# Batch 2's second projection with the weights held still and its result turned by DMA, in a kernel whose whole order is one table, laid anew

## The chip, the cores and the metric

The kernel runs on one core of a Trainium2 chip. The metric is device time in microseconds (us) of one execution. Before the change it is 368.34 us, the median of three runs (368.06 to 368.48).

## What is computed

Attention over 8 batches, 12 heads, 448 positions and 64 values a head, with a denominator that has one extra term; then a gated long convolution over the 448 positions, and a last projection:

```python
scores = q @ k^T / 8
e = exp(scores - max)
attn = e / (sum(e) + exp(-max) + 1e-9)
x = heads side by side of (attn @ v)              # (8, 448, 768)

proj = x @ w_proj                                 # (8, 448, 2304)
x1, x2, x3 = three parts of 768 columns
x2_conv = irfft(rfft(x2) * rfft(filter_fft))      # over the 448 positions
out = (x1 * x2_conv * x3) @ w_out                 # (8, 448, 768)
```

Inputs and output are float32; the kernel computes in bf16 with float32 sums.

## The kernel before

**Attention.** The work runs over 48 head pairs, i = 0 to 47, six for each batch. For a pair, K and Q must stand transposed (tiles kT and qT). In batches 0 and 1 ("staged") this goes: a load of each of k, q and v on SP's queue (L492, L497), casts to bf16 on GpSimd (L519 for k, L525 for q, L532 for v), seven transposes on TensorE (L558 for the shared remainder of K, L560 for k, L567 for q; one group "T" a pair), and copies out of PSUM on VectorE (L577, L588). From batch 2 on ("loaded") the casts go into the tile nat, and DMA transposes on SP's queue (L628, L635) fill qT and kT. The scores come from L867 (two heads side by side on 64 rows each) and L869 (the remainder), the exponentials from ScalarE (L880 and L886), and the sums over v from L898 (remainder) and L906. VectorE divides (L919 to L921) into the tile xb. The tile wout_bf serves as room for the exponentials of pairs 2 and 5 before w_out is loaded into it; so "wout_bf" in an instruction of the first 30 us means pair 2 or 5.

**Dense work of a batch.** xb is transposed into xT (L973 by DMA, L982 on TensorE in batch 0). The gates x1 and x3 are 72 matmuls of 448 columns (L1197). For x2, VectorE folds xT into sums and differences (tile xf, L1046 and L1051), since the transform is done as real matrices on folded halves. Then the second projection has two forms:

- `proj2` (L1074): the folded data is the stationary operand, the weights move: 8 groups (4 parts of the spectrum, 2 halves of the columns) of 6 matmuls with 384 columns. Positions lie on the partitions, as the transform that follows needs them. Each group is copied out of PSUM, on ScalarE (L1088) or VectorE (L1086).
- `still2` (L1096): the weights are the stationary operand and all four parts of the folded data move past them at once: 6 groups of 6 matmuls with 456 columns. The result has channels on the partitions. It is copied out (L1109 on ScalarE, L1107 on VectorE) and turned by two DMA transposes on SP's queue (`turn2`, L1113), of three groups each.

The tuple TURNED (L334) names the batches that use the second form: 3 to 7. The room that the copies write is the batch's own xb for the batches that are not in WHOLE, which are those before 5. After it come the transform (L1149 for the first form, L1145 for the second), the product with the filter's spectrum, the inverse (L1244), the gating, and the last projection (L1010), whose results ScalarE copies out (L1319) and SP stores (L1326, L1329).

**What sets the order.** Every step is a task, added with `plan.add`: engine, estimated cost, what it needs and makes. `Plan.run` plays the tasks through with these estimates. ORDER, a table with one number for each task, in the sequence in which the tasks are added, sorts each engine's tasks; each engine executes its own in that order, and waits where an input is missing. The constants at the head of Plan (L52 to L72: LANDING, DELAY, EARLY, TURN_ROOM and others) are its estimates of transfers. With ORDER given, what is played through decides two things: which of the eight PSUM banks a task gets, and where "fillers" stand: runs of small matmuls on zeros (L1483, method `fillers`) that the plan puts into gaps of TensorE which it expects in the first 44 us:

```python
count = int(self.FILL[2] * (at - end) / 0.056) if end >= self.COLD[0] else -int((end - at) // self.COLD[1])
```

GpSimd also issues the loads of weights: the filter (L761 to L765), w_proj in parts (L845) and w_out (L850).

Of the kernel before, what the change touches and what calls it, by code (L numbers as in the profile page):

```python
# [41 lines left out]
class Plan:  # L42
# [11 lines left out]
    LANDING = 1.89  # L54
    DELAY = (0.87, 3.1)
    EARLY = ((3.0, -0.56), (13.0, 0.95))
    TURN_ROOM = 0.55
# [3 lines left out]
    ORDER = ()  # L61
    OPEN = 8
# [19 lines left out]
    def add(self, eng, cost, want, emit, need=(), make=(), take=(), give=(), dma=0.0, run=256, n=1, after=0.0, begun=(), late=0.0, turn=False, part=None, keep=False, port=False, rows=128):  # L82
        want = self.ORDER[len(self.tasks)] if self.ORDER else want + self.SHIFT.get(part, 0.0)
        if eng == "SP":
            dma *= self.STRETCH
        if eng == "DVE" and port:
            cost += self.SHARED
        self.tasks.append((want, len(self.tasks), eng, cost, emit, need, make, take, give, dma, after, run, n, begun, late, turn, keep, port or eng == "POOL" and not dma, rows))

    def run(self):  # L90
# [37 lines left out]
        def over():  # L128
            return sum(h[1] for h in queues["SP"] if h[2][15]) - self.TURN_ROOM if begin else 0.0

# [7 lines left out]
        def transfers(to):  # L138
            nonlocal clock
            while clock < to:  # L140
# [11 lines left out]
                for e, h in heads.items():  # L152
                    h[1] -= step * h[2][11] / total
                    if h[1] <= 1e-9:
                        queues[e].pop(0)
                        landed[e].extend([clock + self.LANDING + h[2][14]] * h[2][12])
                        done(h[2], clock + self.LANDING + h[2][14], "SP")
            release()
# [60 lines left out]
        while any(queue.values()):  # L219
            moved = False  # L220
            for e in queue:
# [33 lines left out]
                if t[9]:  # L255
                    q = queues["POOL" if e == "POOL" else "SP"]
                    if t[15]:

                        begin[t[1]], free[e] = end, 1e9
                    early, more = self.EARLY[e == "POOL"]  # L260
                    q.append([now + self.DELAY[e == "POOL"] + (more if now < early else 0.0), t[9], t])
                    q.sort(key=lambda h: h[0])
# [53 lines left out]
def kernel(  # L316
# [17 lines left out]
    TURNED = (3, 4, 5, 6, 7)  # L334
# [86 lines left out]
    def stage(g, at, n):  # L421
# [4 lines left out]
    plan = Plan(  # L426
        {
            "e": 6, "er": 2, "e3": 3, "er3": 1, "k0": 2, "q0": 2, "u": 1, "w": 1, "xf": 1,
            "x2": 1, "x2s": 1, "x2b": 2, "xs": 2, "t0": 2, "t1": 2, "yh": 1, "g": 1, "x1": 2, "cr": 2, "cw": 1, "cv": 2, "yT": 1, "yR": 1,
            "os": 3,  # L430
        }
    )
# [1031 lines left out]
    with (  # L1464
# [56 lines left out]
        for (part, ch), at in zip(LOADS, LOAD):  # L1521
# [4 lines left out]
            elif ch is None:  # L1526
                add("POOL", 0.82, at, lambda part=part: wproj_load(part, None), make=[("w", part, 0), ("w", part, 1)], dma=4.9,
                    run=115, late=-0.34, after=at)
# [13 lines left out]
    with (  # L1542
# [6 lines left out]
        for b in range(n_batches):  # L1549
            W["yT", b], W["yR", b // 2] = y, yr  # L1550
            stable(b)
            plan = Plan(plan.size)
# [9 lines left out]
    with tc.manual_schedule(engines={E.PE, E.Pool, E.DVE, E.Activation, E.SP}):  # L1562
        plan = main
# [31 lines left out]
```

## Time and profile before

| | |
|---|---|
| time, median of 3 runs | 368.34 us |
| lowest and highest | 368.06, 368.48 us |
| the profiled execution's own time | 371.93 us |
| its span | 370.1 us |
| TensorE busy | 359.4 us (97%) |
| ScalarE, VectorE, GpSimd busy | 262.3, 259.7, 112.0 us |
| granted clock of TensorE, mean | 0.995 |

The span runs from the first to the last instruction; 1.8 us of the execution's own time lie outside it. That execution took 3.6 us more than the median of the others, so durations read from it are those of a slightly slower run. Names stand as written tile, arrow, read tiles; PE is TensorE, PEld its weight loads, ACT ScalarE, DVE VectorE, POOL GpSimd, SP the engine that issues most transfers; a "q" behind the name marks the engine's instruction sequencer.

### The profile page before, as it was taken

Reading aid. Unit: us, or ns where it says so; the run is one execution under the profiler, and the core shown is the slowest. Engines: PE = TensorE matmul, PEld = TensorE weight load, DVE = VectorE, ACT = ScalarE, POOL = GpSimd, SP = SyncE. Lnnn points to the kernel's source line nnn. Section 1 sums busy time; section 2 is a strip of 40 time slices with the busy share of each in tenths; the row PEclk is TensorE's granted clock in tenths of the full one; section 3 lists DMA queues with packets and bytes.
Section 4 is the critical chain, followed back from the end, with each engine's and each line's share of the span. In section 5 each row is a group of like instructions: output and inputs, shape, how many; then the busy total and the mean of one; then the engine's idle time right before and its main releaser. Section 6 shows DMA issues by size and latency. Waiting matters only on the chain. (4 is left out here: it accounts for less than half of the span.)

```text
span 370.1 us, 9355 instructions
## 1 busy us (share of the span) xinstructions
PE 359.4 (97%) x3612; PEld 215.7 (58%) x3612; DVE 259.7 (70%) x671; ACT 262.3 (71%) x453; POOL 112.0 (30%) x247
## 2 busy tenths in 40 slices
PE   8879999999999999999999999999999999999995
PEld 6557666556755675655565555655555556565653
DVE  7547589894798578793586768784478858767570
ACT  6958777776887768877687766888588784465523
POOL 7582453224560354435217144410120000000000
PEclk9989999999999999999999999999999999999999
DMA  8999999987997999899999999879952055135125
GB/s 195 263 240 218 218 201 221 206 189 181 227 223 204 247 319 200 204 200 235 228 209 256 255 229 240 220 173 234 220 111 44 2 87 105 67 95 120 43 91 173
DMA packets 132163, 68.41 MB, mean 185 GB/s; under 512 B 88781, under 2 KB 128656, under 8 KB 132112
## 3 DMA queue, kind: packets, MB, share of 16 engines
q1 hardware_dynamic: 127392, 62.11, 73.9%
q0 software_dynamic: 4480, 5.41, 8.6%
q8 instruction: 29, 0.48, 0.5%
q10 hardware_dynamic: 240, 0.23, 0.3%
q14 instruction: 22, 0.18, 0.2%
HBM read 43.86 MB, written 11.01 MB: 148 GB/s over the span
## 5 line engine op out<-in xcount | busy, mean ns | idle before, releaser
L880 ACT ACTIVATE e<-psum 128x896 bf16<-128x896 f32 x138 | 122.2, 922 | 30.2 <-PE psum L867 29.5
L1197 PE MATMUL psum<-xT,wproj_bf 128*128 128x448 bf16 x576 | 121.5, 352 | 0.0
L1197 PEld LDWEIGHTS <-wproj_bf 128*128 128x128 bf16 x576 | 53.9, 98 | 47.7 <-issue 4.2
L1010 PE MATMUL psum<-wout_bf,yT 128*128 128x384 bf16 x288 | 54.0, 326 | 0.1
L906 PE MATMUL psum<-vn,e 128*128 128x65 bf16 x1104 | 44.3, 194 | 0.0
L906 PEld LDWEIGHTS <-e 128*128 128x128 bf16 x1104 | 39.4, 98 | 6.7 <-issue 3.0
L867 PE MATMUL psum<-qT,kT 64*128 64x448 bf16 x288 | 42.6, 357 | 0.1
L664 POOL CAST nat<-nat 112x512 bf16<-112x512 f32 x36 | 23.2, 651 | 62.8 <-DMA nat<-in_q_dram 62.5
L1157 ACT CAST xs<-psum 113x384 bf16<-113x384 f32 (+1 forms) x64 | 29.2, 486 | 17.5 <-PE psum L1145 10.8
L1319 ACT COPY osb<-psum 128x384 f32<-128x384 f32 x56 | 25.7, 489 | 18.8 <-PE psum L1010 11.1
L1163 DVE TENSOR_TENSOR t<-xs,hrs 113x768 bf16<-113x768 bf16 (+1 forms) x64 | 37.7, 612 | 1.7 <-ACT xs L1157 1.6
L1010 PEld LDWEIGHTS <-yT 128*128 128x128 bf16 x288 | 27.3, 98 | 18.4 <-issue 1.1
L1096 PE MATMUL psum<-xf,wproj_bf 128*128 128x456 bf16 x180 | 37.5, 356 | 0.0
L921 DVE TENSOR_TENSOR xb<-psum,den 128x512 bf16<-128x512 f32 x48 | 33.2, 691 | 1.7
L1213 DVE TENSOR_TENSOR g<-x,psum 128x448 bf16<-128x448 bf16 x42 | 25.8, 616 | 10.3 <-PE psum L1197 7.7
L1211 ACT CAST x<-psum 128x448 bf16<-128x448 f32 x42 | 22.3, 541 | 10.9 <-PE psum L1197 9.9
L1253 ACT CAST cr<-psum 128x452 bf16<-128x452 f32 x48 | 24.7, 549 | 7.5 <-PE psum L1244 7.0
L886 ACT ACTIVATE er<-psum 128x448 bf16<-128x448 f32 x46 | 25.3, 556 | 4.1 <-PE psum L869 4.0
L684 POOL CAST nat<-nat 128x384 bf16<-128x384 f32 x29 | 16.0, 558 | 39.2 <-DMA nat<-in_k_dram 33.5
L1074 PE MATMUL psum<-wproj_bf,xf 128*113 128x384 bf16 x144 | 27.1, 328 | 0.0
L1096 PEld LDWEIGHTS <-wproj_bf 128*128 128x128 bf16 x180 | 17.0, 98 | 16.3 <-issue 1.5
L919 DVE TENSOR_SCALAR den<-psum 128x8 f32<-128x8 f32 x48 | 7.9, 164 | 25.0 <-PE psum L906 23.6
(136 smaller groups left out, 491.8 us busy)
## 6 DMA issues: line engine op xcount, KB each, us to landing
nat<-in_q_dram SPq DMA_DIRECT2D x47, 224.0 KB, 4.5
out_dram<-osb SPq DMA_DIRECT2D x23, 384.0 KB, 3.6
nat<-in_k_dram SPq DMA_DIRECT2D x41, 192.0 KB, 4.5
nat<-in_v_dram SPq DMA_DIRECT2D x41, 192.0 KB, 4.5
wproj_bf<-in_moe_w_proj_dram POOLq DMA_DIRECT2D x2, 1152.0 KB, 12.2
out_dram<-osb SPq DMA_DIRECT2D x10, 192.0 KB, 3.2
rests<-in_k_dram SPq DMA_DIRECT2D x8, 192.0 KB, 4.2
rests<-in_v_dram SPq DMA_DIRECT2D x8, 192.0 KB, 4.8
```

The source lines that it names most:

```text
L867: nc.tensor.matmul(sc[:, u, 0:S], kT[b % 2][c, hp, t, :], qT[b % 2][c, hp, :])
L880: nc.scalar.activation(to, of, AF.Exp, scale=SCALE)
L906: nc.tensor.matmul(out_bank(u)[:, n, :], P["e"][1 + t][:, u * S + n * 128 : u * S + n * 128 + 128], vn[b % 2][:, hp, 4 * u + t, :], start= ...
L921: nc.vector.tensor_tensor(W["xb", b][:, hp].rearrange("p n (u d) -> p u n d", u=2), op[:, :, :, 0:DH], rec[:].unsqueeze(3).to_broadcast([1 ...
L1010: nc.tensor.matmul(ops[:n, :DCH], y[:, dt, 0:n], wout_bf[:, dt, ch * DCH : (ch + 1) * DCH], start=(dt == 0), stop=(dt == NDT - 1),)
L1074: nc.tensor.matmul(pps[:FQ, :DCH], W["xf", b][:, kt, pg, 0:FQ], wproj_bf[:, kt, D + ch * DCH : D + (ch + 1) * DCH], start=(kt == 0), stop= ...
L1096: nc.tensor.matmul(pps, wproj_bf[:, kt, D + dt * 128 : D + (dt + 1) * 128], W["xf", b][:, kt], start=(kt == 0), stop=(kt == NDT - 1),)
L1157: nc.scalar.copy(L["xs", par, ch][:K, pg % 2, :], L["Z", pg, ch][:K, :DCH])
L1163: nc.vector.tensor_tensor(t[:K], L["xs", par, ch][:K], h, op=ALU.mult)
L1197: nc.tensor.matmul(p[:, :S], wproj_bf[:, kt, 2 * part * D + dt * 128 : 2 * part * D + (dt + 1) * 128], xT()[:, kt, 0:S], start=(kt == 0), ...
L1213: nc.vector.tensor_tensor(g[:, dt, :], L["x1", dt], p[:, :S], op=ALU.mult)
L1319: nc.scalar.copy(L["os", st][:n, ch * DCH : (ch + 1) * DCH], L["O", st, ch][:n, :DCH])
```

## The change

Three things are changed. Batch 2 joins TURNED, so its second projection is of the second form: `still2` and two DMA transposes for `proj2`. The estimates of transfers are renewed: four constants, and a table TIMES that gives 254 tasks, those that start transfers, a cost, transfer time, weight and lateness of their own. And ORDER has new numbers throughout (2,134 for 2,136, since batch 2 has other tasks).

```diff
-    LANDING = 1.89
-    DELAY = (0.87, 3.1)
-    EARLY = ((3.0, -0.56), (13.0, 0.95))
-    TURN_ROOM = 0.55
+    LANDING = 1.738
+    DELAY = (0.917, 3.66)
+    EARLY = ((3.0, -0.67), (13.0, 0.95))
+    TURN_ROOM = 1.05
...
+    TIMES = {}
...
+        cost, dma, run, late = self.TIMES.get(len(self.tasks), (cost, dma, run, late))
         self.tasks.append((want, len(self.tasks), eng, cost, emit, need, make, take, give, dma, after, run, n, begun, late, turn, keep, port or eng == "POOL" and not dma, rows))
...
-    TURNED = (3, 4, 5, 6, 7)
+    TURNED = (2, 3, 4, 5, 6, 7)
...
-    plan.ORDER = (2, 0, 1, 152, 3, 4, 0, 0, 2, 1, 3, 4, 2, 9, 32,
...
+    plan.ORDER = (2, 0, 2, 167, 3, 4, 0, 0, 2, 1, 3, 4, 3, 1, 30,
...
+    plan.TIMES = {3: (0.64, 0.05, 256.0, 0.0), 15: (0.58, 0.735, 50.0, 0.1807), 16: (0.58, 1.17, 50.0, -0.1523),
...
```

Lines behind L437 move down by 4: L845 becomes L849. In the main part TensorE has 48 matmuls of L1074 less and 36 of L1096 more, and 78 fillers where there were 72. VectorE loses four copies of L1086 and gets three of L1107, ScalarE loses four of L1088 and gets three of L1109, and SP gets two DMA transposes of L1113 more.

**GpSimd, from the cast of k for pair 3 on.** L519 is a cast of k, L525 one of q, each for the next pair in turn; L532 is one of v. Before:

```order
L519 CAST ldm<-nat 128x2x3x64
L525 CAST ldm<-nat 112x2x4x64
L761 DMA filt<-in_moe_filter_fft_dram 112x4x768
L762 DMA filt<-in_moe_filter_fft_dram 1x3x768
L765 DMA filt<-in_moe_filter_fft_dram 1x16x48
L525 CAST ldm<-nat 112x2x4x64
L532 CAST vn_93<-nat 128x3x64 x2
L519 CAST ldm<-nat 128x2x3x64 x2
L525 CAST ldm<-nat 112x2x4x64
L845 DMA wproj_bf<-in_moe_w_proj_dram 128x6x768
```

The cast of q right behind the filter's loads is pair 4's, and the two casts of k further on (x2) are those of pairs 4 and 5. After:

```order
L529 CAST ldm<-nat 112x2x4x64 x2
L536 CAST vn_93<-nat 128x3x64 x4
L556 CAST vn_93<-rests 128x6x64
L765 DMA filt<-in_moe_filter_fft_dram 112x4x768
L766 DMA filt<-in_moe_filter_fft_dram 1x3x768
L769 DMA filt<-in_moe_filter_fft_dram 1x16x48
L523 CAST ldm<-nat 128x2x3x64
L536 CAST vn_93<-nat 128x3x64 x2
L849 DMA wproj_bf<-in_moe_w_proj_dram 128x6x768
L536 CAST vn_93<-nat 128x3x64 x2
L523 CAST ldm<-nat 128x2x3x64
L529 CAST ldm<-nat 112x2x4x64 x2
```

The cast of k for pair 3 (the first L523 here) now stands behind the filter's loads, that of pair 4 (the second) ahead of its q, and the first load of w_proj ahead of pair 4's casts, where it stood behind those of pairs 4 and 5.

**TensorE, at the transposes of pair 4** (ks and ldm hold the casts of k and q). Before, the instructions ahead of them are fillers:

```order
L1483 LDWEIGHTS idle
L1483 MATMUL psum<-idle 128x128
L558 LDWEIGHTS ks
L558 MATMUL psum<-ident_bf,ks 128x128
L560 LDWEIGHTS ldm
L560 MATMUL psum<-ident_bf,ldm 128x128
```

After, half of pair 2's sums over v stands there, which used to follow:

```order
L910 LDWEIGHTS wout_bf
L910 MATMUL psum<-vn_93,wout_bf 128x65
L562 LDWEIGHTS ks
L562 MATMUL psum<-ident_bf,ks 128x128
L564 LDWEIGHTS ldm
L564 MATMUL psum<-ident_bf,ldm 128x128
```

Counted over the whole order, 44 of the 72 fillers stood ahead of pair 4's transposes and 28 behind them; now 71 of the 78 stand ahead and 7 behind. Ahead of pair 3's transposes there were 36, and there are 69.

**SP, at batch 2's two new transposes** (L1117, into the tile x). Before, at this place in the queue:

```order
L679 DMA nat<-in_k_dram 128x2x192 x2
L1326 DMA out_dram<-osb 128x768
L973 DMA_TRANSPOSE xT<-xb 128x12x128
L658 DMA nat<-in_q_dram 112x2x256
L679 DMA ks<-in_v_dram 128x2x192
L658 DMA nat<-in_q_dram 112x2x256
L679 DMA nat<-in_v_dram 128x2x192
L679 DMA nat<-in_k_dram 128x2x192
```

After:

```order
L662 DMA nat<-in_q_dram 112x2x256
L683 DMA nat<-in_v_dram 128x2x192
L1117 DMA_TRANSPOSE x_2362<-xb 128x12x128
L977 DMA_TRANSPOSE xT<-xb 128x12x128
L1117 DMA_TRANSPOSE x_2362<-xb 128x12x128
L662 DMA nat<-in_q_dram 112x2x256 x2
L683 DMA nat<-in_v_dram 128x2x192 x2
L639 DMA_TRANSPOSE kT_89<-nat 128x12x128
```

The two stand on either side of a transpose of xb, and loads of q, k and v for later pairs are queued behind them. Up to the transfers that were issued around 50 us, SP's queue holds the same loads in the same order as before.

3 lines of the change are left out of this document (2 added, 1 removed).

## Prediction

> **What bounds the kernel now.** I read the page first, then the waits of TensorE, then windows and timelines of the first 47 us, and last the places where batch 2 and batch 3 do their second projections. The page:
>
> ```profile
> span 370.1 us, 9355 instructions
> ...
> PE 359.4 (97%) x3612; PEld 215.7 (58%) x3612; DVE 259.7 (70%) x671; ACT 262.3 (71%) x453; POOL 112.0 (30%) x247
> ...
> PE   8879999999999999999999999999999999999995
> ```
>
> TensorE is the bound: busy 97%, and its row of 40 slices is full from the fourth slice (28 us) to the last. So only two things shorten the span: less work on TensorE, or less lost in the first slices. Its waits say where the loss is:
>
> ```profile
> PE psum L560 <- POOL ldm L519: 2.3, 1, 2.3
> ...
> PE psum L898 <- POOL vn L552: 0.9, 1, 0.9
> ...
> PE psum L869 <- DMA kT<-nat: 0.4, 1, 0.4
> ```
>
> The largest is one wait of 2.3 us for a cast on GpSimd. The stretches around it (each row: from and to, length, busy us of each engine with instruction counts, then granted clock, DMA share, GB/s), and three stretches of the middle:
>
> ```profile
> 18.00:20.50 2.50, 0.18 (x4) 0.00 (x2) 0.51 (x2) 0.82 (x2) 1.71 (x5) 1.00 1.25 222
> 20.50:22.30 1.80, 1.80 (x31) 1.47 (x32) 0.97 (x3) 0.86 (x2) 1.80 (x4) 0.96 1.12 224
> 22.30:25.60 3.30, 3.30 (x41) 2.04 (x39) 1.94 (x6) 1.95 (x4) 2.71 (x6) 0.50 1.13 282
> 25.60:29.00 3.40, 3.40 (x53) 2.24 (x53) 2.38 (x8) 3.05 (x5) 2.06 (x6) 1.00 1.16 207
> ...
> 130.00:160.00 30.00, 30.00 (x319) 18.63 (x316) 24.20 (x59) 23.18 (x42) 15.80 (x33) 1.00 1.05 242
> 160.00:190.00 30.00, 29.62 (x283) 15.93 (x281) 19.12 (x51) 21.25 (x36) 8.25 (x19) 1.00 1.03 221
> ```
>
> Right behind the wait TensorE runs 3.30 us at a granted clock of 0.50: busy all the time, at half its rate. So the wait costs twice: 2.33 us of idleness, and 3.30 x 0.5 = 1.65 us of slowness. The middle is full, with the DMA engines full too (share above 1).
>
> **What the wait is made of.** GpSimd, then TensorE (timeline: start, length, instruction, idle time before it and what ended it):
>
> ```profile
> 12.20 0.51 POOL L552 CAST vn<-rests 128x384 bf16<-128x384 f32 x1 [0.88 <-DMA rests<-in_v_dram]
> ...
> 14.25 0.96 POOL L761 DMA_DIRECT2D filt<-in_moe_filter_fft_dram  x1
> ...
> 18.79 0.62 POOL L525 CAST ldm<-nat 112x512 bf16<-112x512 f32 x1 [2.51 <-DMA nat<-in_q_dram]
> 19.35 0.65 POOL L532 CAST vn<-nat 128x192 bf16<-128x192 f32 x2
> 19.93 0.97 POOL L519 CAST ldm<-nat 128x384 bf16<-128x384 f32 x2
> ...
> 21.39 1.73 POOL L845 DMA_DIRECT2D wproj_bf<-in_moe_w_proj_dram  x2
> ...
> 17.51 0.61 PE L1483 MATMUL psum<-idle 128*128 128x128 bf16 x8
> 17.96 0.22 PE L558 MATMUL psum<-ident_bf,ks 128*128 128x128 bf16 x1
> 20.50 0.34 PE L560 MATMUL psum<-ident_bf,ldm 128*128 128x128 bf16 x3 [2.33 <-POOL ldm L519]
> ```
>
> Pair 4's q lands at 18.79. GpSimd, which executes in order, casts it, then v, and only then pair 4's k; TensorE's transposes start at 20.50. Everything behind them on TensorE waits too, and ScalarE with it (the first row is the first score of a remainder, which (c) below uses):
>
> ```profile
> 8.85 0.36 PE L869 MATMUL psum<-qT,kT 128*128 128x448 bf16 x1
> ...
> 7.87 2.62 ACT L880 ACTIVATE e<-psum 128x896 bf16<-128x896 f32 x3 [1.75 <-PE psum L867]
> ...
> 21.44 0.92 ACT L880 ACTIVATE e<-psum 128x896 bf16<-128x896 f32 x1 [2.62 <-PE psum L867]
> ...
> 36.87 3.38 PE L1197 MATMUL psum<-xT,wproj_bf 128*128 128x448 bf16 x17
> ```
>
> The stretch ends where the first gate starts, at 36.87; from there on TensorE has enough work.
>
> **The change, part by part.** First the projection of batch 2. The clean runs of both forms, each with the start of what follows:
>
> ```profile
> 45.02 2.11 PE L1074 MATMUL psum<-wproj_bf,xf 128*113 128x384 bf16 x12
> 46.97 0.22 PE L558 MATMUL psum<-ident_bf,ks 128*128 128x128 bf16 x1
> ...
> 168.55 3.63 PE L1096 MATMUL psum<-xf,wproj_bf 128*128 128x456 bf16 x18
> 172.11 0.36 PE L867 MATMUL psum<-qT,kT 64*128 64x448 bf16 x2
> ...
> L1096 PE MATMUL psum<-xf,wproj_bf 128*128 128x456 bf16 x180 | 37.5, 356 | 0.0
> ...
> L1074 PE MATMUL psum<-wproj_bf,xf 128*113 128x384 bf16 x144 | 27.1, 328 | 0.0
> ```
>
> Start to start, a matmul of the first form takes (46.97 - 45.02)/12 = 0.163 us, one of the second (172.11 - 168.55)/18 = 0.198 us. 48 x 0.163 = 7.8 us go, 36 x 0.198 = 7.1 us come: 0.7 us less. By the groups' busy time it is 48 x 27.1/144 - 36 x 37.5/180 = 9.0 - 7.5 = 1.5 us, but busy time counts each group's drain beside the next group's start. Of 0.7 and 1.5 I take 0.9, nearer to the spacing. All of it is on the path, since TensorE is full there. Four copies of about 0.5 us become three of about 0.6 on each of ScalarE and VectorE, which are at 71 and 70%: nothing.
>
> The two DMA transposes have a price of their own. Batch 3's, which exist already:
>
> ```profile
> 173.17 1.76 SPq L1113 DMA_TRANSPOSE x<-xb  x1
> ...
> DMA to landing us min/median/max: 3.7/4.3/5.2
> ...
> 178.84 0.34 PE L1145 MATMUL psum<-x,ft 113*112 113x384 bf16 x1
> ```
>
> From the third group's last matmul (172.11) to the transform (178.84) lie 6.7 us, filled with other matmuls, and no wait of TensorE is put down to these transposes. Batch 2's now have a like distance: between its third group and its transform the new order puts 18 more matmuls of L1096 (18 x 0.198 = 3.6 us), six of L1197 and the scores and sums of attention pairs, much as stands there for batch 3. So the latency is covered. If the cover failed by one landing, it would cost up to 4.3 us. What is not covered is that the transposes, 3.5 us of SP's queue, stand ahead of loads of q, k and v in the stretch where the DMA share is 1.05, and TensorE has already waited 0.4 us for a kT there. I price this and the middle's new order at +0.4, that one wait again, with bounds of 0 and 2.4 (the half of a landing more).
>
> The renewed transfer times execute nothing; they have moved PSUM banks, fillers, and with ORDER the order. The bigger part is therefore the order of the first 37 us.
>
> (a) The wait for pair 4. Its k is now cast ahead of its q, so the transposes can start 0.62 us after q lands, at 19.4 if it lands as before: 1.1 us sooner. But the filter's loads now follow the cast that ended at 12.71, 1.5 us before 14.25, and run beside this very load, which may land up to as much later. The gain is between 0 and 1.1. Half of pair 2's sums now stands ahead of the wait, about 0.6 us of work. In sum 0.6 to 1.7 less; I take 0.8.
>
> (b) The half clock. 27 more fillers stand ahead of these transposes (71 for 44), so TensorE is kept busy where it idled 2.33 us. If that idleness is what brought the clock to 0.50, the 1.65 us go. The Trainium skill ("TensorE: Matmul & The Clock Gate", Part 1: The HAM clock gate) says that the clock falls back to half after an idle window of about 3.4 us, in windows that run on their own. Here 2.33 us of idleness were enough, and the slow stretch is one such window long. By the rule taken strictly the wait would not be the cause, the fillers would cure nothing, and the sum would be 1.65 us less of a gain. I go by the row.
>
> (c) What is paid for it. ScalarE's first exponential (7.87) is now the remainder's, whose score stands behind pair 1's transposes and began at 8.85: about 1 us later, of which ScalarE's gain in (a) takes back a part. The first w_proj load goes out some 5 us sooner than 21.39, beside the loads for pairs 4 to 7; its price is the last rival's, at most 2.5 us. Between 0 and 2.5; I take 0.8.
>
> The sum: -0.9 (projection) + 0.4 (transposes and middle) - 0.8 (a) - 1.65 (b) + 0.8 (c) = -2.15 us. The profiled execution would go from 371.93 to 369.8 us, with a span near 368.0. It is 3.6 us slower than the median of the runs, so I can't exclude that its wait is larger than theirs; I set the same difference on the median: 368.34 - 2.15 = 366.2.
>
> **Rivals.** *The early gain does not come through.* The wait moves to pair 3, ahead of whose transposes 69 fillers now stand; or the half clock comes whatever TensorE does; or TensorE arrives sooner in the middle, where DMA is full and kT lands just in time, and waits there for what it won. Only the projection is left: 368.34 - 0.9 = 367.4. For it speaks the share above 1 up to 190 us; against it that TensorE waited only once, 0.4 us, for a kT.
>
> *The early stretch closes up.* All of (a), 1.7, and (b), nothing paid in (c), and the 21 fillers that no longer stand behind pair 4's transposes (28 before, 7 now) leave no gap: at (17.96 - 17.51)/8 = 0.056 us each, 1.2 us. With the projection 1.7 + 1.65 + 1.2 + 0.9 = 5.45: 362.9. Against it: loads share the same full DMA engines.
>
> *Slower: the early w_proj load holds up pairs 5 to 7.* Its size and time to landing:
>
> ```profile
> wproj_bf<-in_moe_w_proj_dram POOLq DMA_DIRECT2D x1, 1152.0 KB, 13.5
> ```
>
> At the 224 GB/s of the row above its 1152 KB are 5.1 us of all DMA engines. If half of it goes ahead of the loads of k and q for pairs 5 and 6, these land 2.5 us later; TensorE waits for them as it did for pair 4, and the clock falls again. Then (a) and (b) bring nothing, 2.5 us come on top, and with -0.9 and +0.4 the time is 368.34 + 2.0 = 370.3. It decides once pair 5's or 6's transposes start over 2 us later than pair 4's plus the work between. For it: the DMA share is 1.12 to 1.25 there already, and in the profile q for pair 4 came last. Against it: the gate can't start before this load has landed, 21.39 + 13.5 = 34.9, so sooner is what the gate needs. The Trainium skill ("DMA: Bandwidth & Descriptors", Issuing engines are not separate DMA queues) states the mechanism: transfers issued by different engines run on the same 16 DMA engines and interleave. The trace's shares agree.
>
> **How the numbers follow.** The forecast as summed gets 0.46, the early gain that does not come through 0.23, the early stretch that closes up 0.13, the slower case 0.18. About 0.2% of the time, 0.74 us, is what a measurement of this kernel can tell from no change. 367.4 lies at this border: I count half of its case as faster. Faster 0.46 + 0.13 + 0.11 = 0.70, within 0.2% 0.12, slower 0.18. The likeliest case alone, with the bounds of (a) to (c), is 364.5 to 368.1; for 8 in 10 the range reaches toward both outer cases: 363.4 to 369.6.
>
> **What would show it.** In the profile after: no single wait of TensorE over 1 us between 10 and 37 us, and a granted clock of 1.00 from 20 to 30 us; the first gate (now L1201) at 34 to 36 us in place of 36.87; L1100 x216 and L1078 x96 with the same spacings; TensorE's row full in the middle, with no wait over 0.5 us for kT or for the tile x. I am wrong if a half-clock stretch shows up again, if the gate starts no sooner, or if a wait for transfers of over 1 us stands behind 100 us.

## The result, and the profile after

The changed kernel takes 374.05 us (median of 18 runs, 372.16 to 376.92), the one before 368.51 beside it: a ratio of 1.0136, 95% interval 1.0115 to 1.0156. It is 1.4% slower. The profiled execution took 376.92 us with a span of 375.0; the profiled one of before took 371.93 with 370.1.

The page of the kernel after, in the rows that were read before:

```profile
span 375.0 us, 9333 instructions
PE 360.8 (96%) x3606; PEld 213.5 (57%) x3606; DVE 259.1 (69%) x670; ACT 262.4 (70%) x452; POOL 111.4 (30%) x247
PE   7975899999999999999999999999999999999995
PEclk9995999999999999999999999999999999999999
```

TensorE's row is full again, but from the sixth slice (47 us) on instead of the fourth, and the clock's row has a 5 in the fourth slice (28 to 37 us). Its waits (total, times, longest):

```profile
PE psum L562 <- POOL ks L551: 4.4, 1, 4.4
PE psum L1495 <- DVE idle L1483: 1.1, 1, 1.1
PE psum L564 <- POOL ldm L523: 1.0, 1, 1.0
PE psum L871 <- DVE qT L592: 1.0, 1, 1.0
PE psum L902 <- ACT er L890: 0.6, 1, 0.6
PE psum L1014 <- issue: 0.6, 1, 0.6
```

The 2.3 us for pair 4's cast are gone. In their place stand 4.4 us for another cast, `ks`: batch 1's shared remainder of K, which the transposes of pair 6 read, and behind it 1.0 us for pair 6's own k. The timeline of after shows the place on GpSimd, SyncE and TensorE:

```profile
13.11 0.96 POOL L765 DMA_DIRECT2D filt<-in_moe_filter_fft_dram  x1
...
17.36 0.89 POOL L849 DMA_DIRECT2D wproj_bf<-in_moe_w_proj_dram  x1
...
29.19 0.51 POOL L551 CAST ks<-rests 64x384 bf16<-64x384 f32 x1 [8.30 <-DMA rests<-in_k_dram]
...
14.26 0.45 SPq L513 DMA_DIRECT2D rests<-in_k_dram  x1
...
19.39 0.34 PE L564 MATMUL psum<-ident_bf,ldm 128*128 128x128 bf16 x3
...
26.64 0.40 PE L986 MATMUL psum<-ident_bf,xb 128*128 128x128 bf16 x4
31.45 0.29 PE L562 MATMUL psum<-ident_bf,ks 128*128 128x128 bf16 x1 [4.41 <-POOL ks L551]
32.78 0.50 PE L564 MATMUL psum<-ident_bf,ldm 128*128 128x128 bf16 x3 [1.04 <-POOL ldm L523]
...
42.27 3.38 PE L1201 MATMUL psum<-xT,wproj_bf 128*128 128x448 bf16 x17
```

In the trace of before the same cast and the load that it needs stand here:

```profile
24.34 0.50 POOL L547 CAST ks<-rests 64x384 bf16<-64x384 f32 x1 [0.59 <-DMA rests<-in_k_dram]
...
14.00 0.41 SPq L509 DMA_DIRECT2D rests<-in_k_dram  x1
```

SyncE issues the remainder at about the same time in both, 14.0 and 14.3 us. Its rows among the DMA issues, with the time from issue to landing in us, before and after:

```profile
rests<-in_k_dram SPq DMA_DIRECT2D x1, 192.0 KB, 10.2
```

```profile
rests<-in_k_dram SPq DMA_DIRECT2D x1, 192.0 KB, 14.8
```

So the cast starts at 24.34 and at 29.19. What differs is who is on the DMA engines. Per queue (packets, MB, share of 16 engines' time), in the window from 24 to 26 us before,

```profile
q1 hardware_dynamic: 499, 0.45, 93.7%
q0 software_dynamic: 43, 0.06, 16.2%
```

and from 26 to 28 us after, the last window of the stretch from 22 to 28 in which it looks like this:

```profile
q0 software_dynamic: 204, 0.31, 85.4%
q1 hardware_dynamic: 204, 0.14, 29.5%
```

q0 carries GpSimd's loads (the filter and w_proj), q1 those that SyncE issues (q, k, v and the remainders). Both queues send as many packets, 204 and 204, but a packet of q0 is 1.5 KB and one of q1 0.7 KB, and q0's takes three times as long: while both have work, the loads get 0.14 MB in 2 us instead of 0.45. The Trainium skill ("DMA: Bandwidth & Descriptors", Queues, rings and completion order) says that each DMA engine takes its queues in turn, a whole packet from each; the equal counts agree, as far as the Trainium skill and the profile mean the same by a packet.

Last the clock. Stretches of after, each as long as a window or three (from and to, length, busy us of each engine, granted clock, DMA share, GB/s):

```profile
25.16:28.57 3.41, 1.88 (x22) 0.97 (x18) 3.27 (x9) 3.25 (x5) 0.00 (x0) 1.00 1.15 225
28.57:38.81 10.24, 6.32 (x75) 4.28 (x76) 2.16 (x5) 2.49 (x5) 6.25 (x14) 0.50 1.09 224
38.81:42.22 3.41, 3.41 (x38) 2.21 (x36) 2.94 (x10) 3.25 (x9) 1.19 (x3) 1.00 1.18 278
```

Half clock lasts 10.24 us, three times the 3.41 of before (22.17 to 25.58), and costs half of the 6.32 us in which TensorE was busy: 3.2 us. The first gate starts at 42.27 instead of 36.87, 5.4 us later. From there to the end of the span it is 332.7 us after and 333.2 before, and no wait behind it is longer than a microsecond: the whole loss lies ahead of the gate.

### The profile page after: what moved, and what is told of

The parts are those of the page before. It is cut to its first block, busy times and chain, and to the rows that moved or that the text cites. A ratio compares the mean times of both kernels' runs of the same rounds, so it can differ in the third digit from the quotient of the medians.

```text
span 375.0 us, 9333 instructions
## 1 busy us (share of the span) xinstructions
PE 360.8 (96%) x3606; PEld 213.5 (57%) x3606; DVE 259.1 (69%) x670; ACT 262.4 (70%) x452; POOL 111.4 (30%) x247
## 5 line engine op out<-in xcount | busy, mean ns | idle before, releaser
L1201 PEld LDWEIGHTS <-wproj_bf 128*128 128x128 bf16 x576 | 54.1, 98 | 48.3 <-issue 4.3
L910 PE MATMUL psum<-vn,e 128*128 128x65 bf16 x1104 | 45.5, 195 | 0.0
L1100 PE MATMUL psum<-xf,wproj_bf 128*128 128x456 bf16 x216 | 44.9, 356 | 0.0
L910 PEld LDWEIGHTS <-e 128*128 128x128 bf16 x1104 | 40.4, 98 | 7.2 <-issue 1.9
L1161 ACT CAST xs<-psum 112x384 bf16<-112x384 f32 (+1 forms) x64 | 29.5, 488 | 12.4 <-PE psum L1149 8.1
L1167 DVE TENSOR_TENSOR t<-xs,hrs 113x768 bf16<-113x768 bf16 (+1 forms) x64 | 36.3, 582 | 2.6 <-ACT xs L1161 2.6
L1014 PEld LDWEIGHTS <-yT 128*128 128x128 bf16 x288 | 26.5, 98 | 19.9 <-issue 3.4
L668 POOL CAST nat<-nat 112x512 bf16<-112x512 f32 x36 | 24.0, 670 | 41.7 <-DMA nat<-in_q_dram 41.5
L700 POOL CAST vn<-nat 128x192 bf16<-128x192 f32 x58 | 22.1, 411 | 37.5 <-DMA nat<-in_v_dram 37.4
L1100 PEld LDWEIGHTS <-wproj_bf 128*128 128x128 bf16 x216 | 20.5, 98 | 19.1 <-issue 1.1
```

The source lines that it names most:

```text
L910: nc.tensor.matmul(out_bank(u)[:, n, :], P["e"][1 + t][:, u * S + n * 128 : u * S + n * 128 + 128], vn[b % 2][:, hp, 4 * u + t, :], start= ...
L1014: nc.tensor.matmul(ops[:n, :DCH], y[:, dt, 0:n], wout_bf[:, dt, ch * DCH : (ch + 1) * DCH], start=(dt == 0), stop=(dt == NDT - 1),)
L1100: nc.tensor.matmul(pps, wproj_bf[:, kt, D + dt * 128 : D + (dt + 1) * 128], W["xf", b][:, kt], start=(kt == 0), stop=(kt == NDT - 1),)
L1161: nc.scalar.copy(L["xs", par, ch][:K, pg % 2, :], L["Z", pg, ch][:K, :DCH])
L1167: nc.vector.tensor_tensor(t[:K], L["xs", par, ch][:K], h, op=ALU.mult)
L1201: nc.tensor.matmul(p[:, :S], wproj_bf[:, kt, 2 * part * D + dt * 128 : 2 * part * D + (dt + 1) * 128], xT()[:, kt, 0:S], start=(kt == 0), ...
```

## The experiments

Theory after this reading: **the early w_proj load holds up the loads behind it**, the third rival's mechanism. Rivals: the filter's earlier loads or the new order of the casts (A), and batch 2's projection or the middle (B). All times are medians; "ratio" is against the kernel before, run beside it, with its 95% interval. The ratio is not the quotient of the two medians and differs from it here by up to 0.25%. Where an edit below changes the order on an engine, the fillers, which the kernel lays into the gaps of its plan, change in number too (a filler takes 0.056 us); such a difference is named where it matters.

**Where w_proj's load stands.** On GpSimd, in the kernel after (w0_late; no other engine's order moves):

```diff
-L849 DMA wproj_bf<-in_moe_w_proj_dram 128x6x768
 L536 CAST vn_93<-nat 128x3x64 x2
 L523 CAST ldm<-nat 128x2x3x64
 L529 CAST ldm<-nat 112x2x4x64 x2
 L523 CAST ldm<-nat 128x2x3x64
+L849 DMA wproj_bf<-in_moe_w_proj_dram 128x6x768
```

> One instruction moves: on GpSimd the first load of w_proj goes from behind v of pair 3 to behind k of pair 5, where the kernel before had it, some 4 us later; every other engine's order is the same. Theory (the load holds up the loads behind it): while w_proj moves, its queue has 85 to 90% of the DMA engines and the loads of pair 6 about a quarter of their usual rate; issued later, it leaves them a gap after the filter. Batch 1's K remainder lands by 25 us instead of 29, the wait of 4.4 us shrinks below 1 us, the clock is at half for one window of 3.4 us or none instead of 10.2 us, and the time goes from 374.0 to 366.5 - 368.5 us. Rival A (the filter's earlier loads, or GpSimd's new order of casts, hold up pair 6): wait and time stay, 373 - 374.5. Rival B (the loss is in batch 2's projection or the middle): the wait may shrink, the time stays above 372.

Measured: 369.22 us, ratio 1.0008 (0.9985 to 1.0031). One moved instruction takes back 4.8 of the 5.5 us. The timeline of w0_late:

```profile
19.32 0.89 POOL L849 DMA_DIRECT2D wproj_bf<-in_moe_w_proj_dram  x1
...
24.45 0.50 POOL L551 CAST ks<-rests 64x384 bf16<-64x384 f32 x1 [4.24 <-PE psum L910]
...
26.71 0.23 PE L562 MATMUL psum<-ident_bf,ks 128*128 128x128 bf16 x1 [0.42 <-DVE xT L1047]
...
34.14 3.38 PE L1201 MATMUL psum<-xT,wproj_bf 128*128 128x448 bf16 x17
```

The cast is 4.7 us earlier, the wait 0.4 us, the gate at 34.1. In its DMA queues q0 is nearly silent from 22 to 24 us (0.09 MB against 0.50 of q1): that is the gap in which the remainder lands. The time is above the band that the theory gave (366.5 to 368.5), so something of rival B may be left; TensorE also paused for 0.57 us near the end, which comes up below.

The same load moved the other way in the kernel before (w0_early), from behind q of pair 5 to right behind the filter:

```diff
 L765 DMA filt<-in_moe_filter_fft_dram 1x16x48
+L845 DMA wproj_bf<-in_moe_w_proj_dram 128x6x768
 L525 CAST ldm<-nat 112x2x4x64
 L532 CAST vn_93<-nat 128x3x64 x2
 L519 CAST ldm<-nat 128x2x3x64 x2
 L525 CAST ldm<-nat 112x2x4x64
-L845 DMA wproj_bf<-in_moe_w_proj_dram 128x6x768
```

> The kernel before, with the same one load moved the other way: right behind the filter's loads on GpSimd, near 16.5 us instead of 21.4. Nothing of the change is in it. Theory: K of batch 1's remainder and k of pair 6 land 3 to 5 us later, TensorE waits for the cast of the remainder by 2 to 5 us, the clock falls for longer than one window, and the time goes from 368.4 to 372 - 375 us. Rivals A and B: 367.5 - 369.5, the load alone does little.

Measured: 367.89 us, ratio 0.9972 (0.9949 to 0.9995). The theory as it stood fell: w_proj goes out at 15.9 us, earlier than in the kernel after, and nothing is held up.

```profile
13.90 0.96 POOL L761 DMA_DIRECT2D filt<-in_moe_filter_fft_dram  x1
...
21.90 0.51 POOL L547 CAST ks<-rests 64x384 bf16<-64x384 f32 x1
...
33.34 3.38 PE L1197 MATMUL psum<-xT,wproj_bf 128*128 128x448 bf16 x17
```

Here the remainder's cast comes at 21.9 us, and the remainder itself has landed 8.4 us after its issue. SyncE had issued it at 13.1, ahead of the filter's 13.9, and q0's first packets stand in the trace only from 18 us on. So the remainder had 4.9 us of the engines before q0 moved, and was through soon after. In the kernel after, the remainder goes out at 14.3 and q0's packets start at 16, a start of 1.7 us; in before it is 4.5 us. Mended theory: the remainder has two chances, **a start ahead of the filter's transfer, or the gap between the filter and w_proj**; the change took both. That is tried from both sides.

The kernel before with both loads early (both_early):

```diff
+L761 DMA filt<-in_moe_filter_fft_dram 112x4x768
+L762 DMA filt<-in_moe_filter_fft_dram 1x3x768
+L765 DMA filt<-in_moe_filter_fft_dram 1x16x48
 L532 CAST vn_93<-nat 128x3x64 x2
 L519 CAST ldm<-nat 128x2x3x64
 L525 CAST ldm<-nat 112x2x4x64
-L761 DMA filt<-in_moe_filter_fft_dram 112x4x768
-L762 DMA filt<-in_moe_filter_fft_dram 1x3x768
-L765 DMA filt<-in_moe_filter_fft_dram 1x16x48
+L845 DMA wproj_bf<-in_moe_w_proj_dram 128x6x768
```

> The kernel before with two of GpSimd's loads moved to where the change has them: the filter behind the casts of v of pair 0 and V's remainder (near 12.7 us instead of 14.3), the first w_proj load behind q of pair 3 (near 16.5 us instead of 21). w_proj alone moved did nothing. Theory, mended: K of batch 1's remainder, issued on SyncE at 14 us, has two chances, ahead of the filter's transfer or in the gap between the filter and w_proj; only with both early has it neither. Then its cast comes at 26 to 29 us instead of 22 to 24, pair 6's transposes at 29 to 33 us, and the time is 371 to 375 us. Rival (the rest of the new early order, such as the order of the casts, is needed too): 368 to 369.5 us, cast below 25 us.

Measured: 377.02 us, ratio 1.0201 (1.0133 to 1.0268), in four runs; that is more than was expected (371 to 375).

```profile
13.23 0.96 POOL L761 DMA_DIRECT2D filt<-in_moe_filter_fft_dram  x1
...
16.85 0.89 POOL L845 DMA_DIRECT2D wproj_bf<-in_moe_w_proj_dram  x1
...
28.43 0.50 POOL L547 CAST ks<-rests 64x384 bf16<-64x384 f32 x1 [6.34 <-DVE uw L812]
...
30.72 0.29 PE L558 MATMUL psum<-ident_bf,ks 128*128 128x128 bf16 x1 [0.34 <-POOL ks L547]
```

The remainder went out at 14.28 us and took 14.0 us to land, at 28.28: the cast could not start before that, although the view names work of VectorE, which ended at 28.37. Two loads moved in the kernel before, with its order of casts, its projection and its middle as they were, make the whole loss and more. The edit also laid 28 more fillers in front, at most 1.6 us of TensorE's time, so how much the two loads make by themselves is a little less than the ratio says. The kernel after with the filter behind (filt_late), w_proj right behind it:

```diff
-L765 DMA filt<-in_moe_filter_fft_dram 112x4x768
-L766 DMA filt<-in_moe_filter_fft_dram 1x3x768
-L769 DMA filt<-in_moe_filter_fft_dram 1x16x48
 L523 CAST ldm<-nat 128x2x3x64
 L536 CAST vn_93<-nat 128x3x64 x2
+L765 DMA filt<-in_moe_filter_fft_dram 112x4x768
+L766 DMA filt<-in_moe_filter_fft_dram 1x3x768
+L769 DMA filt<-in_moe_filter_fft_dram 1x16x48
 L849 DMA wproj_bf<-in_moe_w_proj_dram 128x6x768
```

> The changed kernel with the filter's loads moved on GpSimd behind k and v of pair 3, from 13.1 to some 16.5 us; w_proj stays right behind, near 18.5 us instead of 17.4. Mended theory: the remainder of K, issued at 14.3 us, now goes ahead of the filter and lands by 23 us though w_proj follows the filter without a gap; no wait above 1.5 us for its cast, one half-clock window at most, 368 to 370 us. Rival (what counts is w_proj's place alone): the cast stays at 27 to 29 us and the time above 372.

Measured: 369.51 us, ratio 1.0022 (0.9993 to 1.0051), with 22 more fillers; the cast at 23.55 us, as the remainder landed 7.4 us after its issue.

```profile
16.31 0.96 POOL L765 DMA_DIRECT2D filt<-in_moe_filter_fft_dram  x1
...
18.33 0.89 POOL L849 DMA_DIRECT2D wproj_bf<-in_moe_w_proj_dram  x1
...
23.55 0.51 POOL L551 CAST ks<-rests 64x384 bf16<-64x384 f32 x1 [1.70 <-issue]
```

So either load moved back heals it, and neither alone makes it. The landing times go with the ways that are open: 14.8 and 14.0 us in after and both_early, where both loads are early, and 7.4 to 10.9 in before, w0_late, w0_early and filt_late. Rival A in its first form (the filter alone) and rival B as the cause of the loss are out.

**Less ahead of the remainder.** In the kernel after, on SyncE (v4_behind), v of pair 4 goes behind the three loads that pair 6 needs:

```diff
-L501 DMA nat<-in_v_dram 128x2x192
 L496 DMA nat<-in_q_dram 112x2x256
 L513 DMA rests<-in_k_dram 128x6x64
 L501 DMA nat<-in_k_dram 128x2x192
+L501 DMA nat<-in_v_dram 128x2x192
```

> The changed kernel with one load moved on SyncE: v of pair 4 (192 KB) from ahead of q of pair 6, K's remainder and k of pair 6 to behind them. While GpSimd's queue is busy the loads move some 0.12 MB in 2 us, so 192 KB less ahead are up to 3 us: the cast of K's remainder at 26 to 27 us instead of 29.2, the wait 1.5 to 2.5 us instead of 4.4, and the time 370.5 to 372.5 us if v of pair 4 isn't missed itself. If the landing depends on GpSimd's transfers alone and not on what stands ahead in SyncE's queue: 373.5 to 374.5 us.

Measured: 373.47 us, ratio 1.011 (1.0038 to 1.0181), in four runs. A miss, and the timeline says why:

```profile
25.72 0.51 POOL L551 CAST ks<-rests 64x384 bf16<-64x384 f32 x1 [5.87 <-PE psum L871]
...
30.68 0.64 POOL L536 CAST vn<-nat 128x192 bf16<-128x192 f32 x2 [3.77 <-DMA nat<-in_v_dram]
31.27 0.50 POOL L551 CAST ks<-rests 64x384 bf16<-64x384 f32 x1
```

The remainder is cast in two halves, and on GpSimd v of pair 4 stands between them. The first half came 3.5 us sooner, as expected of 192 KB less; then GpSimd waited 3.8 us for the v that had been put behind, with the second half in its queue. A load can't be moved without the cast that waits for it in order.

**The wait and the clock apart.** The kernel after, with fillers where TensorE waits (warm; task 88 is pair 6's transposes, and the fillers use its bank):

```diff
-count = int(self.FILL[2] * (at - end) / 0.056) if ...
+count = 75 if t[1] == 88 else int(self.FILL[2] * (at - end) / 0.056) if ...
...
-]
+] if t[1] != 88 else [(0.0, self.banks[t[7][0]][0])]
```

> The changed kernel with 75 fillers of 0.056 us (4.2 us) ahead of pair 6's transposes, where TensorE waits 4.4 us; nothing else. If the idleness brings the clock down: the transposes start when they did (31 to 33 us), the clock stays at 1.00 up to 40 us, and of the 10.2 us at half clock, 6.5 of them busy, some 3.3 us come back: 370.5 - 371.5. If the clock falls whatever TensorE does: 373.5 - 374.5 with the same half-clock stretch. The rest to 368, the wait itself, stays in both.

Measured: 371.48 us, ratio 1.0064 (1.0039 to 1.0089). Of the granted clocks of its ten runs none is below 0.998; of the 18 of the kernel after, all are 0.995 or less: 12 are at 0.989 to 0.991, which is about two windows of 3.41 us at half clock, four at 0.993 to 0.995 and two, the profiled one among them, at 0.985 and 0.986. The stretches of warm:

```profile
27.00:31.00 4.00, 4.00 (x75) 4.00 (x74) 2.33 (x4) 1.33 (x2) 3.94 (x7) 1.00 1.13 262
31.00:38.00 7.00, 7.00 (x112) 4.83 (x110) 4.88 (x13) 5.40 (x12) 3.53 (x8) 1.00 1.21 241
```

Pair 6's transposes start at 31.04 us, as late as ever, and the clock stays at 1.00. So idleness does bring the clock down, and of the 5.5 us some 2.6 are the clock's and the rest the wait's. By the rule that the prediction quoted from the Trainium skill ("TensorE: Matmul & The Clock Gate", Part 1: The HAM clock gate), that it takes an idle window, fillers would have cured nothing in before; the rows say that less suffices. The window ahead of the fall was busy 1.88 us of 3.41 here (25.16 to 28.57). That the windows have one length and run on their own agrees: 3.41 and 10.24 us.

**The kernel before again, for a second profile** (before_again; no edit).

> The kernel before once more, for a second profile. The first was 371.93 us long at a granted clock of 0.995; of 35 runs only five have such a clock and over 370.3 us, the median is 368.8. Theory (the first profile was not a usual run): no half-clock window, the wait for pair 4's k under 1.5 us instead of 2.3, the first gate at 33 to 35 us instead of 36.9. If the profile was usual: 2 us or more of waiting and a half-clock window of 3.4 us again.

The "five" of this text are four: runs of 370.35, 370.47, 370.88 and 371.44 us at 0.995. Of all 141 runs of before beside these experiments 29 have a clock of 0.996 or less. The second profile (370.52 us) has no half clock and these rows:

```profile
20.10 0.34 PE L560 MATMUL psum<-ident_bf,ldm 128*128 128x128 bf16 x3 [1.53 <-POOL ldm L519]
...
35.01 3.38 PE L1197 MATMUL psum<-xT,wproj_bf 128*128 128x448 bf16 x17
```

The wait for pair 4 is 1.53 us instead of 2.33 and the gate 1.9 us sooner (the wait is a hair over what was expected). The first profile was one of the runs, one in five, that lose a window.

**Step (a) by itself.** The kernel before with pair 4's k cast ahead of its q (k4_first), and the same with w_proj early as in w0_early (both_good):

```diff
+L519 CAST ldm<-nat 128x2x3x64
 L525 CAST ldm<-nat 112x2x4x64
 L532 CAST vn_93<-nat 128x3x64 x2
-L519 CAST ldm<-nat 128x2x3x64 x2
+L519 CAST ldm<-nat 128x2x3x64
```

> The kernel before with one swap on GpSimd, k of pair 4 cast ahead of its q, as the change has it. The prediction's step (a) put 0.8 us on the early wait for pair 4, of which 0.6 by this swap. If the usual run of before waits there: 0.4 to 0.7 us less, 367.9 to 368.3 against 368.6. If that wait is used up by what TensorE waits for right after (q of pair 5, the remainder): no change within 0.3 us.

> The kernel before with this swap and with the first w_proj load right behind the filter's loads, which alone gave 0.28% less. If both work where they are: the first gate at 33 us and 367.0 to 367.8 us, faster than both kernels by 0.2 to 0.4%. If the early load's gain was chance: 368.3 to 368.9.

Measured: 369.00 us, ratio 0.9999 (0.9973 to 1.0026), and 369.38, ratio 1.0018 (0.9996 to 1.004). In the trace of k4_first the wait for pair 4's k is gone, and the gate waits in its place:

```profile
17.76 0.33 PE L560 MATMUL psum<-ident_bf,ldm 128*128 128x128 bf16 x3
...
33.72 3.39 PE L1197 MATMUL psum<-xT,wproj_bf 128*128 128x448 bf16 x17 [0.41 <-DMA wproj_bf<-in_moe_w_proj_dram]
```

In both_good w_proj is early too and that wait is away, but the time is no better. What it gives instead isn't found. w0_early once more (w0_early_b, the same edit):

> The kernel before with the first w_proj load right behind the filter's, once more. If its 0.28% was real: 367.4 to 368.1 against 368.6 for before. If it was chance: 368.3 to 368.9.

Measured: 367.94 us, ratio 0.9982 (0.9959 to 1.0006). Two sets of runs at 367.9 us are the lowest medians of the study; the second interval touches 1.

**Batch 2's projection by itself.** First a cut in time: up to 34 us every engine's order is that of before, from there on that of after (early_old). Its diff is the table of numbers; on GpSimd it puts back, for one,

```diff
+L523 CAST ldm<-nat 128x2x3x64
+L529 CAST ldm<-nat 112x2x4x64
 L765 DMA filt<-in_moe_filter_fft_dram 112x4x768
```

> Every engine's order up to 34 us is that of the kernel before, from there on that of the changed one, with batch 2's projection still and turned. Theory (all of the loss is early): no wait of 4.4 us, one half-clock window as before, and what is left is the projection and the new middle: -0.9 + 0.4 = -0.5 to -1.0 us, 367.3 - 368.2. Rival B: 370 or more.

Measured: 370.03 us, ratio 1.0027 (1.0005 to 1.005). That is above the one band and at the edge of the other (370 or more). The early loss is gone, but the seam has waits that neither kernel has (0.6 us at 40.7 and 0.5 at 41.5 us), and there are 39 more fillers, up to 2.2 us of TensorE's time. So the run says little of the projection. A cleaner one undoes the projection alone (moving), on the base w0_late, run again beside it (w0_late_b); the tables of the order and of the times follow the one line that is shown:

```diff
-TURNED = (2, 3, 4, 5, 6, 7)
+TURNED = (3, 4, 5, 6, 7)
```

> The changed kernel with the first w_proj load back behind k of pair 5, once more, as the base of the next run on the same chip: 368.5 to 369.5 us, as in its first runs.

> That base with batch 2's second projection as it was before the change: 48 matmuls of 384 columns in place of 36 of 456, at the same places of the same order, eight copies in place of six, and no transposes of batch 2 on SyncE. By the prediction's terms (0.9 less for the matmuls, and 0 to 0.4 paid for the transposes) it is 0.5 to 0.9 us slower than its base; in the trace the sum of the matmuls' spacings is 0.7 to 0.9 larger and no new wait of TensorE shows. Rival (the transposes in a full SyncE queue cost what the matmuls gain): the same time as its base, within 0.3 us.

Measured: 369.24 us, ratio 1.0023 (0.9992 to 1.0053), and 368.84, ratio 1.0014 (0.9989 to 1.0039). No difference that can be measured: the rival was right about the time. The matmuls do get cheaper. In the kernel after, batch 2's stand as

```profile
133.79 2.47 PE L1100 MATMUL psum<-xf,wproj_bf 128*128 128x456 bf16 x12
136.19 0.74 PE L871 MATMUL psum<-qT,kT 64*128 64x448 bf16 x6
```

0.200 us each from start to start, so 36 are 7.2 us against 48 x 0.163 = 7.8. Two things stand against it in the traces. One is the cover of the transposes. In w0_late_b, v4_behind and shift, three of the eight profiles so far in which the projection and the transform stand where the change put them, TensorE waits 0.9 to 1.1 us for batch 2's transposes (x<-xb); in before's form there is nothing to wait for. The row of shift, the next kernel:

```profile
141.15 0.53 PE L1149 MATMUL psum<-x,ft 113*113 113x384 bf16 x2 [1.12 <-DMA x<-xb]
```

The other is a pause behind the program's branch, at its end (w0_late_b first, then moving):

```profile
360.12 2.92 PE L1014 MATMUL psum<-wout_bf,yT 128*128 128x384 bf16 x17 [1.14 <-issue]
```

```profile
359.90 5.67 PE L1014 MATMUL psum<-wout_bf,yT 128*128 128x384 bf16 x32
```

"issue" means that the profile shows no releaser. The pause is in after, w0_late, w0_late_b and v4_behind, ahead of the last 17 matmuls each time, and in none of the other profiles so far. These four have a TensorE program of the same length, 7166 instructions ahead of the branch, which itself stands 32 matmuls ahead of the end. Three kernels test that: six fillers more on the base (shift, 7178), twelve fewer on moving (moving_hit, 7166), and six more with the first transform of batch 2 moved back by a gate and an output group (best_new, 7177):

```diff
-count = int(...) if ...
+count = 6 if t[1] == 88 else int(...) if ...                (shift, best_new)
+count = -12 * (t[1] == 451) + int(...) if ...               (moving_hit)
```

> The base (the changed kernel with the first w_proj load behind k of pair 5) with six fillers ahead of pair 6's transposes, 0.34 us in a wait of 0.42 us. If the pause of TensorE near 360 us hangs on where the instructions lie in its program: it is gone from the trace, and the time is 368.1 to 368.7 us against 369.2. If it comes from what the engines do there: it stays at 0.57 us or more and 369 to 369.4 us.

> The base with batch 2's projection undone, and twelve fillers less near 9 us, so that TensorE's program has as many instructions as the base's. If the pause hangs on the program's length: it shows up here too, near 360 us, 0.57 us or more, and the time is 369.3 to 370 us against 368.8 without. If not: no pause, 368.8.

> As shift, and the first transform of batch 2 stands 2.1 us later, behind the gate's and the output's matmuls that followed it (its two copies and one product later too). No wait for batch 2's transposes, no pause at the end: 367.8 to 368.4 us, which would be faster than both kernels by 0.1 to 0.2%. If the time of the base hangs on neither: 369.0 to 369.4.

Measured: shift 369.08 us, ratio 0.9992 (0.9969 to 1.0014), no pause; moving_hit 370.95, ratio 1.005 (1.0021 to 1.0078), with a pause of 0.73 us ahead of the last 17; best_new 371.05, ratio 1.0067 (1.0045 to 1.0088), with one of 1.67 us ahead of the last 22. The pause comes and goes with the length, and 11 instructions more move it 5 matmuls, which are 10 instructions, nearer to the branch: it sits at a fixed place of the program, not of the work. None of the three times was as expected: shift had no pause and was still above its band, and the two with a pause were 0.95 us and more above theirs. In four of moving_hit's 12 runs the clock also lost a window; it has twelve fillers fewer. Two last ones: the length of after on w0_early, by seven fillers fewer (early_hit), and best_new with two fillers more (best_new2, 7181):

```diff
+count = -7 * (t[1] == 458) + int(...) if ...                (early_hit)
+count = 8 if t[1] == 88 else int(...) if ...                (best_new2)
```

> The kernel before with the early w_proj load, and seven fillers less near 9 us, so that TensorE's program has 7166 instructions ahead of its branch, as the changed kernel has, in place of 7180. Nothing else of the change is in it. If the pause hangs on the program's length alone: TensorE pauses 0.6 to 1.1 us ahead of the last 17 matmuls, and the time is 368.6 to 369.2 us against 367.9 without. If it belongs to the changed order: no pause, 367.9.

> best_new (the changed kernel with the first w_proj load late and batch 2's first transform 2.1 us later) with two fillers more, 7181 instructions ahead of the branch in place of 7177, where the pause was 1.67 us. By the lengths so far (pause at 7158, 7166, 7177; none at 7178, 7180, 7186 and above) the pause is gone: 368.0 to 369.0 us against 371.05, and no wait for batch 2's transposes. If best_new's own order is slow: 370 or more.

early_hit has none of the change in it and has the pause:

```profile
360.48 2.92 PE L1010 MATMUL psum<-wout_bf,yT 128*128 128x384 bf16 x17 [0.83 <-issue]
```

It took 368.45 us, ratio 0.9967 (0.9936 to 0.9998); best_new2 has no pause and took 368.89, ratio 0.9978 (0.9953 to 1.0003). That the pause hangs on the length is shown. (The expectation of best_new2 counts k4_first, 7158, among the lengths with a pause; its last 32 matmuls take 5.76 us where others take 5.67, a tenth of a microsecond, which is no such pause.) What it costs isn't settled: 2.1 us between moving and moving_hit and 2.2 between best_new and best_new2, both more than the pause itself, but 0.1 between w0_late and shift, and between w0_early and early_hit 0.5 by the medians and nothing by the ratios. In best_new the time outside the span also grew, from 1.8 us to as much as 3.2.

The lowest ratios are those of early_hit (0.9967) and w0_early (0.9972 and 0.9982), both the kernel before with w_proj's load early: 0.2 to 0.3% below before, which is about the bound of what can be told. For the changed kernel it is best_new2 (0.9978): w_proj late, the transform later, no pause. It beats the kernel after clearly; that it beats before is not shown, as its interval holds 1 and the medians are 368.89 and 369.08 us.

## Why the prediction was wrong, step by step

The forecast was 366.2 us with a range of 363.4 to 369.6; the result is 374.05, outside it, on the side that had a chance of 0.18.

**The step that failed is the price of the early w_proj load in (c)**: "its price is the last rival's, at most 2.5 us", inside a sum of 0.8. The rival itself had the right mechanism, the right place (pair 6's transposes start at 31.45, over 2 us late) and two wrong sizes. "If half of it goes ahead of the loads" shared the DMA engines by bytes; they share by packets, and q0's are three times as long, so the loads fell to a third for as long as q0 had work. And I had w_proj alone. The filter was in the prediction only as something that pair 4's load may run beside; that it closes the way ahead, and w_proj the gap behind, is what both_early and filt_late show. The remainder of K was not in the prediction at all, though pair 6's transposes read it, and GpSimd casts it ahead of pair 6's q in both kernels. So the wait is 4.4 + 1.0 us instead of 2.5, and the clock, which I let fall once more (1.65 us), fell for two windows in most runs and for three in the profiled one (3.2 us).

**(a), the wait for pair 4**, was right as a mechanism: it went from 2.33 to 0.2 us. It is worth nothing that could be measured: k4_first takes it away from before and the time stays within the noise. In the second profile of before the wait is 1.53 us, and in k4_first 0.41 us is waited for at the gate in its place; where the rest went is not shown.

**(b), the half clock**, failed twice. Its cause was right, as warm shows, against the rule taken strictly. But there was nothing to gain: four runs of before in five have no such window. I had seen that the profiled execution was 3.6 us above the median and put the whole difference on the median all the same; the right reading was that the stretch from which (a) and (b) were taken was part of that difference. And the cure, fillers ahead of pair 4's transposes, stood at the wrong wait: the new one at pair 6 had none.

**The projection**, -0.9 us, is right on TensorE (0.6 to 0.7 by the spacings) and does not show in the time. **The transposes and the middle**, +0.4 with an upper bound of 2.4, measured 0 to 1.1 us in the profiles at batch 2's transposes (and 1.3 us once, in w0_late, at batch 4's), and the cover that I counted at "18 more matmuls" fails by about 1 us in three profiles of the eight that have the change's middle. Together they come to about nothing, which was one of the ends. The pause at the end, 0.57 us in after, was in no term.

**The signs I named**: no wait over 1 us before 37 us (there are two), a clock of 1.00 from 20 to 30 us (it falls at 28.57), the gate at 34 to 36 us (42.27) were all wrong. The spacings, the full row and the absence of long waits behind 100 us came as said.

That the sum of the early terms was a gain rested on one profile. Most kernels that keep the remainder's way open, changed or not, lie from 367.9 to 369.5 us; early_old, moving_hit and best_new are at 370.0 to 371.1, for the reasons told above as far as they are known. No kernel here beat before by more than about 0.3%, so little was left to win.

## What to carry to other kernels

When a large load is moved ahead, look at what it will share the DMA engines with packet by packet, and find every load whose consumer has no slack in that stretch, with the gap in which it lands now; a load is hurt when its last gap closes, so test moved loads together and not one by one. Check a stretch on a second profile, or on the granted clocks of all runs, before its waits are taken as something to gain. Where an in-order engine casts what is loaded, the order of the loads and that of the casts have to be moved together.

## What the runs showed of the hardware

While GpSimd's queue and SyncE's both had work, they sent equal numbers of packets, 204 and 204 in 2 us, and the one with the longer packets had 85% of the engines' time. q0's first packets stand in the trace 3 to 4 us behind the issue (13.11 to 16 us in after, 13.90 to 18 in w0_early).

A window of 3.41 us in which TensorE was busy for 1.88 us (25.16 to 28.57 in after) was enough to halve the clock in the next. It came back after one window at half clock that was busy throughout (35.40 to 38.81 in after, 22.17 to 25.58 in before), and not after one busy for 2.62 us (31.98 to 35.40 in after). So half clock is counted in windows: one in some runs of before, mostly two and at times one or three after.

TensorE paused 0.6 to 1.7 us at a fixed place of its program behind the branch, with lengths of 7166 and 7177 instructions ahead of it and not with 7178, 7180, 7181 or 7190. The Trainium skill ("Runtime: NRT & Kernel Launch", Instruction fetch mechanics) says that instructions are fetched in blocks of 256 and that a taken branch can force a fetch. In the traces there are 16 KB transfers on a queue of their own for instructions, and in after the last of them starts at 366.09 us, behind the branch and 2.35 us ahead of the end of the pause (window from 365.44 to 366.44 us; packets, MB, share):

```profile
q8 instruction: 1, 0.02, 7.2%
```

Such a transfer stands behind the branch in the profiles without a pause too, and the trace doesn't say for which engine it is. That the pause is a wait for instructions fits with this, but it is only argued.
